# Gate, gelu and up products of the first two feed-forward groups in three passes instead of chunk by chunk

## The chip, the core and the metric

The kernel runs on one core of a Trainium2 chip. The metric is the device time of one execution, in microseconds (us). The engines are TensorE (PE), VectorE (DVE), ScalarE (ACT), GpSimd (POOL) and SyncE (SP, which issues the transfers). They run on their own and wait for one another by semaphores. Each engine executes its instructions in the order in which the program lists them.

## What is computed

One transformer block with adaptive layer norm: attention with 32 heads of width 16 over 2048 tokens of width 512, and then a gated feed-forward of width 1792.

```python
mod = (_silu(c) @ w_mod).reshape(c.shape[0], 6, 1, -1)     # sa, ca, ga, sb, cb, gb
h = _layernorm(x, axis=-1) * (1 + ca) + sa
x = x + ga * _A_ref(h, A_wqkv, A_wo)                        # softmax attention
h = _layernorm(x, axis=-1) * (1 + cb) + sb
x = x + gb * _B_ref(h, B_w_gate, B_w_up, B_w_down)
# _B_ref: _gelu(x @ w_gate) * (x @ w_up) @ w_down, gelu in its tanh form
```

## The kernel before

**Attention.** The queries are cut into six sets (`SETS`: three of 512 tokens, one of 256, two of 128). Eight head groups (`qd`) of four heads go over each set; one head group of one set is a unit. A unit of 512 queries has 16 rounds, one for each tile of 128 keys, and a round has four score blocks of 128x512, one for each head. PE writes the scores of three blocks into three PSUM banks (`ps_sc`, two such halves, used in turn), and one ACT instruction (line 1387, recorded by line 326) takes their exp into `E`, 1536 columns wide. Then PE multiplies by the values (`pv_mms`) into the accumulator `ps_pv`. At the end of a unit DVE copies the accumulator to `osb`, and the denominators go through DRAM and back by small transfers on SP's queue.

**Rounds on DVE.** Some rounds are taken off ACT. In the last four of the 16 rounds of keys, one bank of the three is given to DVE in four successive iterations; DVE computes the exp in bit arithmetic (line 1394: `dreg<-ps_sc`, `mreg<-ps_sc`, 128x512), and then makes four shifted copies of the whole round (`shift_task`, line 1476: `mreg<-dreg`, `mreg<-mreg`, 128x2048), each with its own value product (`ps_pv<-mreg,vs`). The iteration's exp on ACT is then 1024 wide. A round is started when DVE is free within 700 ns in the planner's model, fewer than `BACK` = 8 operations wait for DVE, and one of three buffers (`kq`) is free (lines 1358 to 1371). It is started at least `AHEAD` = 24 blocks before its turn. After the third set a further condition holds: little side work may be outstanding (`credit < CREDIT`).

**Side work.** Projections, output products and the feed-forward of the sets already finished run between the attention steps on PE, in one PSUM bank (`ps_mi`). They are generators (`plan`, from line 1118), paced by credit so that each is done by a due position in the sequence of score blocks. The feed-forward of group `gi` (`side_ffn`) runs while set `gi + 1` is in attention.

**The planner.** The whole order is fixed when the program is built: `stream` keeps a model of when each engine is free (`model`, `cost`, `probe`) and issues what the model has ready. DVE and ACT operations that are not urgent lie in a list of tasks (`task`); a task may have a condition and sets a key when it is recorded, and a generator may hold until a key is there (`until`). ACT's tasks are emptied ahead of each exp (lines 1385 and 1386). The order of the recorded instructions is the order on the chip; the times of the model are not.

**The feed-forward before.** `G(ci)` multiplies two gate columns blocks of 128 (`fc`), four matmuls of 512 columns each; DVE copies each from `ps_mi` to `g` (in `wreg`). Then four steps follow for the pair, as one task: `w = g*g`, `w = 0.0447 w + 1`, `w = w*g` on DVE, 1024 columns wide, and tanh on ACT. Tanh lies in the table that exp uses. `U(ci)` holds until the tanh is recorded, multiplies the two up blocks, and takes each out of PSUM by `(w + 1) * up` (line 1040); a last DVE product with `g` gives `prod` (line 1042). G of the next pair runs between G and U of a pair. For the first three groups (`flow`) the weights are streamed: gate and up each have two buffers of 256 columns (`wst`, in `mreg`), loaded one pair ahead, and the seven parts of the down weights go to `wdst`, four of which lie in the place of `wst`. Group 3 and later hold the weights in place. The final stage, after the last scores, uses the gelu of ACT itself, which lies in another table.

Of the kernel before, what the change touches and what calls it, by code (L numbers as in the profile page):

```python
# [5 lines left out]
ACT = mybir.ActivationFunctionType  # L6
ALU = mybir.AluOpType
# [6 lines left out]
P = 128  # L14
# [6 lines left out]
NDC = D // P  # L21
NFC = F // P
# [20 lines left out]
NS = 4  # L43
AHEAD = 24
FLOW = 3
URGENT = 9
LATE = 2
EARLY = 2
BACK = 8
END = (0, None)  # L50
# [14 lines left out]
class _Op:  # L65
    __slots__ = ("eng", "stream", "seq", "fn", "inc", "waits", "clock", "tag", "t1")

    def __init__(self, eng, stream, seq, fn):
        self.eng = eng
        self.stream = stream  # L70
        self.seq = seq
        self.fn = fn
        self.inc = False
        self.waits = {}
        self.clock = None
        self.tag = None


class _Recorder:


    def __init__(self, nc):
        self.nc = nc
        self.ops = []
        self.count = {}
        self.bystream = {}
        self.clock = {e: {} for e in ALLENG}
        self.hist = {}
        self.pitch = {}
        self.kind = {}  # L90
        self.sem = {}
        self.dry = False
        self.split = False
        self.probing = None
        self.free = {e: 700.0 for e in ALLENG}
        self.dma_free = self.pe_issue = self.pe_end = 0.0
        self.pe_mode = None
        self.tile_free = [0.0] * 16
        self.log = []

# [218 lines left out]
    def act(self, out, in_, func, bias=None, scale=1.0, accum=None):  # L319
        kw = {} if bias is None else {"bias": bias}  # L320
        wr = [out]
        if accum is not None:
            kw["accum_out"] = accum
            wr.append(accum)
        rd = [in_] + [a for a in (bias, scale) if isinstance(a, bass.AP)]
        return self.rec("act", lambda e: e.activation(out, in_, func, scale=scale, **kw), rd, wr,  # L326
                        cost=self.cost("act", out, [in_], "act"))

    def tt(self, eng, out, a, b, op):
        return self.rec(eng, lambda e: e.tensor_tensor(out, a, b, op), [a, b], [out],  # L330
# [88 lines left out]
class _Kernel(_Recorder):  # L419
# [78 lines left out]

    def prologue(self):
        sp, act, pe, dve, pool = "sp", "act", "pe", "dve", "pool"  # L500
        xv = self.A_x.rearrange("b (t p) d -> p (b t) d", p=P)
        wmv = self.w_mod.rearrange("(a p) n -> p a n", p=P)
        wqv = self.A_wqkv.rearrange("(a p) (k n) -> p a k n", p=P, k=3)
        wq4 = self.wqkv.rearrange("p a (k n) -> p a k n", k=3)
        self.dma(sp, self.xs[:, 0:2, :], xv[:, 0:2, :], "x0")
        self.dma(act, self.crow[0:1, :], self.c, "c")
        self.dma(act, self.xs[:, 2:4, :], xv[:, 2:4, :], "x1")
        for i, q in enumerate((sp, act)):
            self.dma(q, self.wmod[:, :, D * i:D * i + D], wmv[:, :, D * i:D * i + D], "wm%d" % i)
# [459 lines left out]
    def side_ffn(self, gi, part=None):  # L969

        q0, W = SETS[gi]
        n = W // P
        tiles = [q0 // P + i for i in range(n)]
        mi = self.mi[:, :]
        c0 = BCOL[gi]
        prod = self.prodT if W == 512 else self.prodL
        flow = gi < FLOW
        kpb = 512 // W
        chunks = []
        width = max(2, kpb)  # L980
        for a in range(0, NFC, width):
            chunks.append(range(a, min(NFC, a + width)))

        def load(x, ci):
            if flow and ci < len(chunks):
                v = (self.B_w_gate, self.B_w_up)[x].rearrange("(a p) n -> p a n", p=P)
                self.dma("sp", self.wst[x][ci % 2], v[:, :, 2 * P * ci:2 * P * ci + 2 * P], "st%d%d" % (x, ci % 2))

        def load_down(i):
            if flow:  # L990
                v = self.B_w_down.rearrange("(f p) n -> p f n", p=P)
                self.dma("sp", self.wdst[i], v[:, 2 * i:2 * i + 2, :], "sd%d" % i)

        yield from self.until(("ln2", gi))
        if flow:
            load(0, 0)
            load(1, 0)
        else:
            yield from self.until("weights")
        for h in range(2):  # L1000
            yield from self.side_t(lambda t: self.normed(gi, t), n, h,
                                   lambda dc: self.t2T[:, dc, c0:c0 + W], self.modB)

        def up(x, ci, sub):
            for s, fc in enumerate(sub):
                for dci in range(NDC):
                    if flow:
                        lhs = self.wst[x][ci % 2][:, dci, P * (fc % 2):P * (fc % 2) + P]
                    else:
                        lhs = self.up_w((self.wg, self.wu)[x], fc, dci)  # L1010
                    yield W, lambda s=s, lhs=lhs, dci=dci: self.mm(
                        mi[:, W * s:W * s + W], lhs, self.t2T[:, dci, c0:c0 + W], start=(dci == 0), stop=(dci == NDC - 1), whole=W == P)

        def G(ci):
            fcs = chunks[ci]
            m = len(fcs)
            g, w = self.gw[:, ci % 2, 0, 0:m * W], self.gw[:, ci % 2, 1, 0:m * W]
            load(0, ci + 1)
            for b0 in range(0, m, kpb):
                sub = fcs[b0:b0 + kpb]  # L1020
                yield from up(0, ci, sub)
                self.copy("dve", g[:, W * b0:W * (b0 + len(sub))], mi[:, 0:W * len(sub)])
                if b0 + kpb >= m and not self.dry:
                    self.task([lambda: self.tt("dve", w, g, g, ALU.mult),
                               lambda: self.ts("dve", w, w, GELU_C, 1.0, ALU.mult, ALU.add),
                               lambda: self.tt("dve", w, w, g, ALU.mult),
                               ("act", lambda: self.act(w, w, ACT.Tanh, scale=TANH_C0))], ("gelu", gi, ci))
                yield END

        def U(ci):  # L1030
            fcs = chunks[ci]
            m = len(fcs)
            g, w = self.gw[:, ci % 2, 0, 0:m * W], self.gw[:, ci % 2, 1, 0:m * W]
            yield from self.until(("gelu", gi, ci))
            load(1, ci + 1)
            for b0 in range(0, m, kpb):
                sub = fcs[b0:b0 + kpb]
                k = len(sub)
                yield from up(1, ci, sub)
                self.stt(w[:, W * b0:W * (b0 + k)], w[:, W * b0:W * (b0 + k)], 1.0, mi[:, 0:W * k], ALU.add, ALU.mult)  # L1040
                if b0 + kpb >= m:
                    self.tt("dve", prod[:, fcs[0]:fcs[0] + m, c0:c0 + W], w.rearrange("p (k n) -> p k n", k=m),
                            g.rearrange("p (k n) -> p k n", k=m), ALU.mult)
                yield END
        nch = len(chunks) if part is None else part
        for i in range(3):
            load_down(i)
        for ci in range(nch + 1):
            if ci < nch:
                yield from G(ci)  # L1050
                if ci >= nch - 2:
                    load_down(3 + ci - nch + 2)
            if ci >= 1:
                yield from U(ci - 1)
                if ci >= nch - 1:
                    load_down(5 + ci - nch + 1)
        if part is not None:
            yield from self.near_end(gi + 1, 6, self.mi[:, 0:P])
            if not self.dry:
                self.done(("part", gi))  # L1060
            return
        for i in range(n):
            for fc in range(NFC):
                yield 512, lambda i=i, fc=fc: self.mm(
                    mi, prod[:, fc, P * i:P * i + P], (self.wdst if flow else self.wd)[fc // 2][:, fc % 2, :], start=(fc == 0), stop=(fc == NFC - 1))
            self.down_fin(mi, tiles[i])
            yield END
        self.done(("ffn", gi))
# [6 lines left out]
    def urgency(self, tk):  # L1075
# [5 lines left out]
        if tk[1] is None or tk[1][0] != "shift":  # L1081
            return 1
        return 0 if self.plain[tk[1][1]] <= URGENT else 2

# [659 lines left out]
```

## Time and profile before

| | us |
|---|---|
| median of 3 runs | 865.73 (864.06 to 866.16) |
| profiled execution | 862.18 |
| its span, first to last instruction | 860.4 |
| ACT busy | 834.0 |
| PE busy | 797.4 |
| DVE busy | 694.8 |

A line of a group names the kernel's line, the engine, the operation, the tile written and the tiles read with their shapes, the count, then busy time, mean ns of one, and the idle time of the engine ahead of them with what ended it. Line 326 is the helper that records every ACT instruction, line 338, 343, 330 and 347 are DVE's helpers, line 313 that of the matmuls. Counts of the change's operations over the whole run, for three groups of which the change touches two:

| operation | shape | count | mean ns |
|---|---|---|---|
| ACT tanh, `wreg<-wreg` | 128x1024 | 21 | 1157 |
| DVE products, `wreg<-wreg` | 128x1024 | 42 | 680 |
| DVE scale and add, `wreg<-wreg` | 128x1024 | 21 | 421 |
| DVE product to `prod`, `hreg<-wreg` | 128x1024 | 21 | 692 |
| ACT table load | | 2 | 1283 |

The two table loads are at the start and ahead of the final stage. DVE exponentiates 192 + 96 score blocks, which are 72 rounds.

### The profile page before, as it was taken

Reading aid. Unit: us, or ns where it says so; the run is one execution under the profiler, and the core shown is the slowest. Engines: PE = TensorE matmul, PEld = TensorE weight load, DVE = VectorE, ACT = ScalarE, POOL = GpSimd, SP = SyncE. Lnnn points to the kernel's source line nnn. Section 1 sums busy time; section 2 is a strip of 40 time slices with the busy share of each in tenths; the row PEclk is TensorE's granted clock in tenths of the full one; section 3 lists DMA queues with packets and bytes.
Section 4 is the critical chain, followed back from the end, with each engine's and each line's share of the span. In section 5 each row is a group of like instructions: output and inputs, shape, how many; then the busy total and the mean of one; then the engine's idle time right before and its main releaser. Section 6 shows DMA issues by size and latency. Waiting matters only on the chain.

```text
span 860.4 us, 27593 instructions
## 1 busy us (share of the span) xinstructions
PE 797.4 (93%) x12434; PEld 285.5 (33%) x12434; DVE 694.8 (81%) x1339; ACT 834.0 (97%) x748; POOL 4.5 (1%) x12
## 2 busy tenths in 40 slices
PE   7889999999999899899999999999999889998988
PEld 3333332322222222222222222222343233354456
DVE  7865989989889989988899989989987663687255
ACT  6999999999999999999999999999999999999992
POOL 1000000000000000000000000000000000000000
PEclk9999999999999999999999999999999999999999
DMA  9000000000003111210002112120134231500000
GB/s 312 9 26 17 3 9 9 10 9 9 10 4 93 44 45 33 58 33 20 10 15 82 45 32 58 34 58 11 45 92 119 80 81 43 153 11 10 21 5 14
DMA packets 63807, 38.06 MB, mean 44 GB/s; under 512 B 17389, under 2 KB 61546, under 8 KB 63690
## 3 DMA queue, kind: packets, MB, share of 16 engines
q1 hardware_dynamic: 62888, 35.52, 14.8%
q8 instruction: 97, 1.59, 0.8%
q10 hardware_dynamic: 802, 0.79, 0.3%
q14 instruction: 20, 0.16, 0.1%
HBM read 33.68 MB, written 2.61 MB: 42 GB/s over the span
## 4 chain that ended last, share of the span: by engine, by line
ACT 82%; PE 8%; DVE 5%; DMA 3%; SPq 1%; issue 1%; ACTq 0%; DVEq 0%
ACT E L326 79%; PE ps_sc L313 4%; PE ps_mi L313 3%; ACT wreg L326 3%; PE ps_pv L313 1%; DMA rb<-scr_rec 1%; DMA scr_rec<-rden 1%; SPq L376 1%; DVE st L366 1%; DVE hreg L338 1%; DMA xs<-in_A_x_dram 1%; DVE nwt L330 0%; DVE wreg L338 0%; DVE dreg L338 0%; DVE mreg L338 0%
## 5 line engine op out<-in xcount | busy, mean ns | idle before, releaser
L326 ACT ACTIVATE E<-ps_sc 128x1536 bf16<-128x1536 f32 (+2 forms) x698 | 805.5, 1343 | 11.8 <-PE ps_sc L313 11.7
L313 PE MATMUL ps_sc<-qT,kmo 32*128 32x512 bf16 (+2 forms) x1408 | 178.7, 323 | 11.3 <-ACT E L326 9.8
L313 PE MATMUL ps_sc<-qT,kme 32*128 32x512 bf16 (+2 forms) x1344 | 172.8, 331 | 13.8 <-ACT E L326 11.1
L313 PE MATMUL ps_pv<-E,vaug 128*17 128x512 bf16 (+2 forms) x2352 | 171.0, 322 | 2.3 <-DVE vaug L347 1.0
L338 DVE TENSOR_SCALAR dreg<-ps_sc 128x512 uint16<-128x512 f32 x192 | 132.3, 690 | 33.1 <-PE ps_sc L313 30.4
L338 DVE TENSOR_SCALAR mreg<-dreg 128x2048 uint16<-128x2048 uint16 x192 | 124.9, 682 | 0.4 <-PE ps_pv L313 0.4
L313 PE MATMUL ps_mi<-wreg,mreg 128*32 128x512 bf16 (+2 forms) x1504 | 110.3, 370 | 11.6 <-DVE wreg L343 6.6
L313 PE MATMUL ps_pv<-mreg,vs 128*17 128x512 bf16 (+2 forms) x1344 | 100.8, 350 | 1.4 <-DVE mreg L338 1.2
L313 PEld LDWEIGHTS ps_sc<-qT,kmo 32*128 32x128 bf16 x1408 | 48.1, 91 | 125.3 <-ACT E L326 96.4
L313 PEld LDWEIGHTS ps_sc<-qT,kme 32*128 32x128 bf16 x1344 | 45.4, 91 | 130.7 <-ACT E L326 98.9
L313 PEld LDWEIGHTS ps_pv<-E,vaug 128*17 128x17 bf16 x2352 | 52.4, 89 | 85.8 <-issue 60.3
L338 DVE TENSOR_SCALAR mreg<-ps_sc 128x512 uint16<-128x512 f32 x96 | 66.3, 691 | 17.2 <-PE ps_sc L313 15.3
L338 DVE TENSOR_SCALAR mreg<-mreg 128x2048 uint16<-128x2048 uint16 x96 | 63.0, 684 | 0.0
L313 PEld LDWEIGHTS ps_mi<-wreg,mreg 128*32 128x32 bf16 (+1 forms) x1504 | 34.0, 95 | 62.5 <-issue 20.6
L347 DVE CAST wreg<-ps_mi 128x512 bf16<-128x512 f32 x51 | 35.0, 687 | 15.4 <-PE ps_mi L313 14.6
L343 DVE SCALAR_TENSOR_TENSOR wreg<-wreg,ps_mi 128x512 bf16<-128x512 bf16 x51 | 34.9, 685 | 13.4 <-PE ps_mi L313 7.8
L313 PEld LDWEIGHTS ps_pv<-mreg,vs 128*17 128x17 bf16 x1344 | 31.2, 89 | 31.2 <-DVE mreg L338 13.8
L313 PE MATMUL ps_mi<-hreg,wreg 128*32 128x512 bf16 (+1 forms) x496 | 39.5, 377 | 2.2 <-DVE hreg L338 1.0
L313 PE MATMUL ps_mi<-wo,onorm 128*32 128x512 bf16 x480 | 37.8, 383 | 0.1
L330 DVE TENSOR_TENSOR wreg<-wreg 128x1024 bf16<-128x1024 bf16 (+1 forms) x60 | 35.7, 603 | 0.7
L330 DVE TENSOR_TENSOR onorm<-osb,rb 128x512 bf16<-128x512 f32 (+2 forms) x43 | 23.5, 548 | 12.1 <-DMA rb<-scr_rec 11.8
L313 PE MATMUL ps_mi<-mreg,hreg 128*32 128x512 bf16 x384 | 32.5, 384 | 0.0
(147 smaller groups left out, 571.0 us busy)
## 6 DMA issues: line engine op xcount, KB each, us to landing
mreg<-in_B_w_up_dram SPq DMA_DIRECT2D x25, 256.0 KB, 3.2
mreg<-in_B_w_gate_dram SPq DMA_DIRECT2D x21, 256.0 KB, 3.0
rb<-scr_rec SPq DMA_DIRECT2D x96, 32.0 KB, 1.8
mreg<-in_B_w_down_dram SPq DMA_DIRECT2D x12, 256.0 KB, 2.7
dreg<-in_B_w_down_dram SPq DMA_DIRECT2D x9, 256.0 KB, 3.7
mreg<-in_w_mod_dram SPq DMA_DIRECT2D x1, 2048.0 KB, 11.5
out_dram<-xs SPq DMA_DIRECT2D x15, 128.0 KB, 1.7
xs<-in_A_x_dram SPq DMA_DIRECT2D x3, 512.0 KB, 8.2
```

The costliest lines, as they stand in the source:

```text
L313: return self.rec("pe", lambda e: e.matmul(out, lhsT, rhs, start=start, stop=stop, tile_position=tp), [lhsT, rhs], [out], cost=(n, int(rhs ...
L326: return self.rec("act", lambda e: e.activation(out, in_, func, scale=scale, **kw), rd, wr, cost=self.cost("act", out, [in_], "act"))
L330: return self.rec(eng, lambda e: e.tensor_tensor(out, a, b, op), [a, b], [out], cost=self.cost(eng, out, [a, b], "tt"))
L338: return self.rec(eng, lambda e: e.tensor_scalar(out, a, s1, s2, **kw), rd, [out], cost=self.cost(eng, out, [a], "ts") + (60 if len(rd) > ...
L343: return self.rec("dve", lambda e: e.scalar_tensor_tensor(out, a, s, b, op0=op0, op1=op1), rd, [out], cost=self.cost("dve", out, [a, b], " ...
L347: return self.rec(eng, lambda e: e.tensor_copy(out, in_), [in_], [out], cost=self.cost(eng, out, [in_], "ts"))
L366: return self.rec("dve", lambda e: e.bn_stats(out, in_), [in_], [out], cost=self.cost("dve", out, [in_], "bn"))
L376: return e.dma_start(out, in_)
```

## The change

For groups 0 and 1 (`gi < BATCH`), `side_ffn` no longer alternates G and U. A new generator, `batch`, goes over all seven pairs of gate blocks first; each block is copied by DVE from PSUM straight to its place in `prod`. When the last of the 14 is recorded, two ACT tasks are entered, each a gelu in place over seven blocks (128x3584). Then all seven pairs of up blocks follow; each block is taken out of PSUM by one DVE operation, `(up * 2) * prod`, in place. The up block `fc` holds until its half's gelu is recorded. The down products are as before.

The four `wst` buffers form one ring for the 14 loads, each issued two pairs ahead. The first two loads are issued behind the first three parts of the down weights, and the transposes of the group's input are moved into `batch`. Group 2 and later are as before. The planner's model adds 1290 ns where ACT goes from exp or tanh to gelu or back.

```diff
+BATCH = 2
...
-        return self.rec("act", lambda e: e.activation(out, in_, func, scale=scale, **kw), rd, wr,
-                        cost=self.cost("act", out, [in_], "act"))
+        cost = self.cost("act", out, [in_], "act")
+        if self.probing is None and func in (ACT.Exp, ACT.Tanh, ACT.Gelu_apprx_tanh):
+            if self.table not in (None, func == ACT.Gelu_apprx_tanh):
+                cost += 1290
+            self.table = func == ACT.Gelu_apprx_tanh
+        return self.rec("act", lambda e: e.activation(out, in_, func, scale=scale, **kw), rd, wr, cost=cost)
...
+        def batch():
+            nch = len(chunks)
+            flat = [self.wst[1][1], self.wst[1][0], self.wst[0][1], self.wst[0][0]]
+
+            def load_n(i):
+                if i < 2 * nch:
+                    v = (self.B_w_gate, self.B_w_up)[i // nch].rearrange("(a p) n -> p a n", p=P)
+                    c = 2 * P * (i % nch)
+                    self.dma("sp", flat[i % 4], v[:, :, c:c + 2 * P], "st%d%d" % divmod(i % 4, 2))
+
+            def act(a, b):
+                return ("act", lambda: self.act(prod[:, a:b, :], prod[:, a:b, :], ACT.Gelu_apprx_tanh))
+            load_n(0)
+            load_n(1)
+            for h in range(2):
+                yield from self.side_t(lambda t: self.normed(gi, t), n, h,
+                                       lambda dc: self.t2T[:, dc, 0:W], self.modB)
+            for i in range(2 * nch):
+                x, ci = divmod(i, nch)
+                load_n(i + 2)
+                for fc in chunks[ci]:
+                    if x:
+                        yield from self.until(("gelu", gi, fc * 2 // NFC))
+                    for dci in range(NDC):
+                        yield W, lambda i=i, fc=fc, dci=dci: self.mm(
+                            mi, flat[i % 4][:, dci, P * (fc % 2):P * (fc % 2) + P], self.t2T[:, dci, 0:W], start=(dci == 0), stop=(dci == NDC - 1))
+                    if x:
+                        self.stt(prod[:, fc, :], mi, 2.0, prod[:, fc, :], ALU.mult, ALU.mult)
+                    else:
+                        self.copy("dve", prod[:, fc, :], mi)
+                        if fc == NFC - 1 and not self.dry:
+                            for j in range(2):
+                                self.task([act(NFC // 2 * j, NFC // 2 * j + NFC // 2)], ("gelu", gi, j), self.after([("mid", gi)]))
+                            self.done(("mid", gi))
+                    yield END
+                if i >= 2 * nch - 4:
+                    load_down(i - 2 * nch + 7)
...
+        if gi < BATCH:
+            yield from batch()
+        for ci in range(nch + 1 if gi >= BATCH else 0):
```

## The prediction

> **What bounds the kernel now.** I read four views: the page's busy shares and the chain of waits, then the busy time by stretches, then ScalarE's (ACT) groups and timeline, then VectorE's (DVE) groups in the stretches that the change touches.
>
> ```profile
> PE 797.4 (93%) x12434; PEld 285.5 (33%) x12434; DVE 694.8 (81%) x1339; ACT 834.0 (97%) x748; POOL 4.5 (1%) x12
> ...
> ACT 82%; PE 8%; DVE 5%; DMA 3%; SPq 1%; issue 1%; ACTq 0%; DVEq 0%
> ```
>
> ```profile
> 268.00:396.00 128.00, 117.99 (x1452) 34.44 (x1451) 115.70 (x192) 127.98 (x117) 0.00 (x0) 1.00 0.17 48
> 396.00:466.00 70.00, 68.21 (x847) 19.42 (x847) 62.47 (x114) 69.99 (x65) 0.00 (x0) 1.00 0.08 21
> 480.00:592.00 112.00, 104.43 (x1285) 29.72 (x1281) 100.87 (x166) 112.00 (x102) 0.00 (x0) 1.00 0.15 41
> ```
>
> The columns of the stretches are PE, weight load, DVE, ACT and POOL busy, the clock, DMA share, GB/s. The gate/up work of the first two groups lies in 268-396 and 480-592 (that is where their 14 tanhs are); 396-466 has only down and output products. ACT is busy for the whole of all three (127.98 of 128, 69.99 of 70, 112.00 of 112), so here a microsecond of ACT is a microsecond of the kernel and nothing else is. DVE is at 90%, 89% and 90%: near full, and that matters for one reason only. The planner gives DVE whole rounds of four score blocks, exponentiated there by bit arithmetic, when DVE is free in its model. Each round is taken off ACT. So DVE time is worth ACT time at an exchange rate, and the change is a trade: it makes ACT dearer directly and gives DVE time back.
>
> **ACT's prices.**
>
> ```profile
> 316.62 1.16 ACT L326 ACTIVATE wreg<-wreg 128x1024 bf16<-128x1024 bf16 x1
> 317.57 2.47 ACT L326 ACTIVATE E<-ps_sc 128x1024 bf16<-128x1024 f32 x2
> 319.80 1.17 ACT L326 ACTIVATE wreg<-wreg 128x1024 bf16<-128x1024 bf16 x1
> ```
>
> ```profile
> 834.05 2.90 ACT L326 ACTIVATE E<-ps_sc 128x1536 bf16<-128x1536 f32 x2
> 836.71 0.75 ACT L326 ACTIVATE wreg<-wreg 128x512 bf16<-128x512 bf16 x1
> 837.23 1.57 ACT L326 ACTIVATE E<-ps_sc 128x1536 bf16<-128x1536 f32 x1
> 838.82 1.28 ACT L326 ACT_TABLE_LOAD   x1
> 840.11 0.20 ACT L326 ACTIVATE tcol<-tcol 128x1 f32<-128x1 f32 x1
> ```
>
> Columns: start, duration, then the instruction. Neighbours overlap, so what one costs is the distance to the next start. A 1536-wide exp: (836.71 - 834.05)/2 = 1.33 us. The pair at 317.57 is one exp of each width (2.23 us), so the 1024-wide one costs 2.23 - 1.33 = 0.90: **0.43 us for a block of 512**. A 1024-wide tanh: 317.57 - 316.62 = 0.95; the 512-wide one 837.23 - 836.71 = 0.52, again 0.43 per 512. The last three lines are the only switch from the exp table to the gelu table: without it the next start would be 837.23 + 1.33 = 838.56, with it 840.11, so **a switch costs 1.55 us**: the 1.28 us load and the lost overlap.
>
> Removed: 14 tanhs x 0.95 = -13.3 us. Added: 4 gelus of 7 x 512 = 3584 columns. No row has that width; from 1024 up by five blocks, 0.95 + 5 x 0.43 = 3.10, four of them 12.4. That gelu runs at the tanh's pace is taken from the final stage, where its 512-wide gelus take 0.60 us beside 0.59 for a plain copy of the same width. Added: switches. Both halves become ready at one point (all gate chunks recorded), and the planner empties ACT's task list before the next exp, so the two stand back to back: one switch in, one out, per group: 4 x 1.55 = 6.2. The switch back to exp has no row: below by the bare load (4 x 1.28 = 5.1), above by the same 1.55 (the load has to wait for the end of the gelu as it did for the exp). I take the upper, it is the one whole switch that was measured. **ACT's direct sum: -13.3 + 12.4 + 6.2 = +5.3 us** (from +4.2).
>
> The Trainium skill (ScalarE: Activation LUTs, "What ACT_TABLE_LOAD costs") speaks against this change: 1283 ns of load and about 1380 ns of drain, 2.66 us for every switch, while exp and tanh share a table. The load agrees with the 1.28 above; the drain doesn't: the activation behind the load starts 0.01 us after its end. By the page the switches would be an estimated 10.6 us, and the direct sum +9.7.
>
> **DVE's prices.**
>
> ```profile
> L338 DVE TENSOR_SCALAR dreg<-ps_sc 128x512 uint16<-128x512 f32 x38 | 26.2, 690 | 5.8 <-PE ps_sc L313 5.5
> L338 DVE TENSOR_SCALAR mreg<-dreg 128x2048 uint16<-128x2048 uint16 x36 | 23.6, 682 | 0.0
> L338 DVE TENSOR_SCALAR mreg<-ps_sc 128x512 uint16<-128x512 f32 x20 | 13.8, 690 | 2.8 <-PE ps_sc L313 2.3
> L338 DVE TENSOR_SCALAR mreg<-mreg 128x2048 uint16<-128x2048 uint16 x20 | 13.1, 686 | 0.0
> ...
> L330 DVE TENSOR_TENSOR wreg<-wreg 128x1024 bf16<-128x1024 bf16 x14 | 9.3, 679 | 0.1
> L330 DVE TENSOR_TENSOR hreg<-wreg 128x1024 bf16<-128x1024 bf16 x7 | 4.8, 692 | 0.2
> ...
> L338 DVE TENSOR_SCALAR wreg<-wreg 128x1024 bf16<-128x1024 bf16 x7 | 2.9, 419 | 0.0
> ```
>
> These are DVE's groups in 268-396. The last three are what goes: 9.3 + 4.8 + 2.9 = 17.0 us a group. All rows of the stretch add up to 124.4 us where 115.7 were busy, since neighbours overlap; at that ratio (0.93) it is 15.8 us, 31.6 for both. What stays is equal in number and price: one copy a gate chunk (684 ns) and one product with the PSUM an up chunk (683), now on the product tile. The four upper rows are the rounds: 58 exps and 56 shifts for 76.7 us, at 0.93 some 5.0 us a round. A round takes four blocks off ACT: 4 x 0.43 = **1.7 us**. So the freed DVE time could buy 31.6/5.0 = 6.3 rounds at most.
>
> Not all of it is to be had. The first up product is put into DVE's queue as soon as its matmuls are issued, and then waits for the first gelu: 1.55 + 3.10 us after ACT reaches it, less about 1 us for the matmuls and the copy ahead: some 3.5 us in which everything behind it on DVE waits (the shifts, the copies of finished accumulators, PE's value products on shifted rounds). Against that stand the waits for tanh that go (1.4 and 1.2 us in the two stretches). ACT itself does not starve: both halves of its score banks are filled before the gelus end.
>
> How many rounds DVE then takes I read from the middle stretch, whose other work is like what is left:
>
> ```profile
> L338 DVE TENSOR_SCALAR dreg<-ps_sc 128x512 uint16<-128x512 f32 x26 | 18.0, 691 | 4.0 <-PE ps_sc L313 3.7
> ...
> L338 DVE TENSOR_SCALAR mreg<-ps_sc 128x512 uint16<-128x512 f32 x12 | 8.3, 691 | 2.6 <-PE ps_sc L313 2.3
> ```
>
> 38 exps, 9.5 rounds in 70 us: one each 7.4 us, with other work at 24% of DVE's time. In 268-396 it is 14.5 rounds, one each 8.8 us, with other work at 35%; without the removed operations that is 22%. During the gelus and switches (2 x 3.10 + 2 x 1.55 = 9.3 us) no scores advance and no round starts. So the first stretch, some 130 us long, holds (130 - 9)/7.4 = 16.4 rounds, +1.9; the second, 112 us with 12.5 rounds now, (115 - 9)/7.4 = 14.3, +1.8. I take **4 more rounds**, between 0 and 6.3: 4 x 1.7 = -6.8 us.
>
> Costed at nothing: PE's four more value products a round (ps_pv<-mreg,vs, 100.8 us for 1344 matmuls, 16 a round: 1.2 us each, 5 in all), which lie beside an ACT that never waits; without that cover they are +5. The weight loads are as many as before, in another order: the down weights now go ahead of the first gate chunk on SP's queue, 3 us each to land, and only side work waits. The planner now also counts a table load at the start of the final stage, which may reorder it: between -1.3 and +1.3 (one load), taken as 0.
>
> **The sum.** +5.3 - 6.8 = **-1.5 us**. The profiled execution took 862.2 us (860.4 span and 1.8 around it), so 860.7 by that; it is 3.5 us below the median of the three runs, 865.7, and I put the forecast on the median: **864.2 us**. A measurement here tells 0.3%, 2.6 us, from no change.
>
> **The rivals.**
> A, *DVE's time converts fully*: all of the 31.6 us turns into 6.3 rounds, 1.7 x 6.3 = 10.7 less, 5.3 - 10.7 = -5.4: 860.3. For it: DVE fills to 90% in each stretch whatever else it does. Against: the wait for the gelu.
> B, *slower: the buffers decide, not DVE's time*. A round holds one of three buffers until its five value products are done, which needs its head pair's turn; and a round must be started 24 blocks ahead. So about three fit into a head pair's 64 blocks. Counting shifted products between accumulator copies, the pairs of 268-396 took 2, 3, 3, 3, 2 and those of 396-466 4, 3, 3: not far apart. If the buffers bind, only 0 to 2 more rounds are had and +5.3 is paid: +1.9 to +5.3, with one round +3.6: 869.3. It decides below 5.3/1.7 = 3.1 more rounds.
> C, *switching costs twice*: an exp comes between the two halves, 8 switches in place of 4: +6.2 on the forecast, 870.4. Against it: the emptying of the task list. The skill's drain would give nearly the same (an estimated +4.4).
>
> **Chances.** Forecast 40% (3 to 5 rounds: 862.5 to 865.9), A 22%, B 31%, C 7%. Faster by over 0.3%: A and the forecast's upper end, 0.31; slower: B below two rounds (0.24) and C, 0.31; within: 0.38. The range reaches to A and, above, to B's one round: 860.5 to 869.5.
>
> **What would show it.** Six table loads in place of two, four of them in two pairs round two gelus of 3.1 us each; DVE stalled 3 to 4 us behind the first; 76 rounds in place of 72 (304 score exps on DVE, now 192 + 96); ACT busy all through. Under 75 rounds B is right. I am wrong altogether if ACT shows idle time in the middle stretches, or if the rounds change after 660 us.

## The result and the profile after

| | before | changed |
|---|---|---|
| median, runs of one comparison | 864.98 us (9 runs) | 869.70 us (9 runs) |
| ratio | | 1.0052, 95% interval 1.0039 to 1.0065 |
| mean granted PE clock, run by run | 0.992 to 1.000 (the 67 runs beside the experiments below) | 0.977 to 0.988 |
| rounds on DVE | 72 | 75 |

The kernel became 4.7 us slower where 1.5 us faster was forecast. Ratios here and below leave out the runs of a second, slower state, so they are not exactly the quotients of the medians. The profiled execution of the changed kernel is its slowest, 874.2 us; its span is 872.5, 12.1 more than before. The profiled execution of the kernel before, 862.2 us, is under all nine runs of the comparison. So the two profiles lie further apart than the medians: they show where time goes, and not how much of the 4.7 us each place has. The busy shares and the chain on the page of the changed kernel:

```profile
PE 812.8 (93%) x12424; PEld 287.5 (33%) x12424; DVE 680.2 (78%) x1307; ACT 835.7 (96%) x742; POOL 4.5 (1%) x12
...
ACT 70%; PE 22%; DVE 5%; DMA 2%; issue 1%; SPq 0%; ACTq 0%; DVEq 0%
```

ACT's busy time grew by 1.7 us only; PE's share of the chain went from 8% to 22%. About the same three stretches of the work as before, moved by what they grew, the middle one taken further (before, ACT was busy for 20.00 of 20 us in 460 to 480, too) (columns: PE, weight load, DVE, ACT and POOL busy, clock, DMA share, GB/s):

```profile
268.00:396.00 128.00, 121.72 (x1472) 35.11 (x1472) 108.89 (x179) 127.26 (x113) 0.00 (x0) 0.97 0.15 42
396.00:480.00 84.00, 81.61 (x943) 22.42 (x947) 71.72 (x131) 79.66 (x73) 0.00 (x0) 0.94 0.11 31
480.00:600.00 120.00, 113.80 (x1324) 30.64 (x1312) 97.89 (x159) 114.18 (x101) 0.00 (x0) 0.91 0.15 41
```

Two things are to be seen. ACT is no longer busy throughout: 0.7, 4.3 and 5.8 us are idle, where it was full before. And the clock column, which was 1.00 in all three, is 0.97, 0.94 and 0.91. ACT's gelus in the first group, from its timeline:

```profile
318.64 1.28 ACT L332 ACT_TABLE_LOAD   x1
319.93 6.27 ACT L332 ACTIVATE hreg<-hreg 128x3584 bf16<-128x3584 bf16 x2
326.21 1.28 ACT L332 ACT_TABLE_LOAD   x1
327.50 2.79 ACT L332 ACTIVATE E<-ps_sc 128x1536 bf16<-128x1536 f32 x2
```

The block is as predicted: two gelus of 3.14 us each back to back, one load on either side, 8.86 us from the first load to the next exp (9.1 with the lost overlap ahead of it). What follows it was not. The second group's block in windows of 3.41 us, the grid on which the clock moves in the records:

```profile
521.60:525.01 3.41, 3.41 (x50) 1.11 (x47) 3.03 (x6) 3.38 (x3) 0.00 (x0) 1.00 0.05 10
525.01:528.42 3.41, 1.83 (x28) 0.54 (x28) 2.23 (x5) 3.41 (x2) 0.00 (x0) 1.00 0.03 2
528.42:531.83 3.41, 0.74 (x8) 0.00 (x0) 0.00 (x0) 3.39 (x4) 0.00 (x0) 0.50 0.43 115
531.83:535.24 3.41, 3.36 (x22) 0.50 (x22) 1.98 (x3) 2.60 (x3) 0.00 (x0) 0.50 0.04 12
535.24:548.90 13.66, 13.66 (x92) 2.35 (x88) 6.46 (x10) 9.72 (x9) 0.00 (x0) 0.50 0.06 17
548.90:552.31 3.41, 3.25 (x36) 0.81 (x32) 2.67 (x5) 2.87 (x4) 0.00 (x0) 1.00 0.00 0
```

In the second window PE is busy 1.83 of 3.41 us, and from the third on its clock is at 0.50, for 20.5 us. PE is then busy all the time (13.66 of 13.66) at half its rate, and it is ACT that waits for scores: it is busy for only 9.72 of 13.66 us. Why PE ran dry, in its timeline of that place:

```profile
526.83 0.39 PE L314 MATMUL ps_mi<-wreg,mreg 128*32 128x512 bf16 x4
528.02 1.15 PE L314 MATMUL ps_mi<-wreg,mreg 128*32 128x512 bf16 x12 [0.80 <-DVE hreg L348]
531.88 1.03 PE L314 MATMUL ps_sc<-qT,kme 32*128 32x512 bf16 x3 [2.72 <-ACT E L332]
```

While ACT is in the block no bank of scores comes free. The side bank is taken by an up block of which 12 of 16 matmuls are issued: the side work's credit was spent, and an open accumulation can take nothing else. So PE waits for the next exp, from 529.2 to 531.9. In the first group the side bank waits for the first product, and so for the first gelu, from 321.9 to 324.0; there the clock is at one half from 323.6 to 330.4.

The planner has a means against this that the text so far did not need: where PE's work in the last 3.413 us is under `FILL` = 4200 columns, it issues filler products on the identity, into a free bank (before, lines 1354 and 1433; 112 of them in the program). Full rate is taken here as 8192 columns in that time, 512 in 0.213 us; in the timelines one group of four quarter matmuls of 512 columns follows the other after 0.216 us. Through the gelus there is hardly a free bank. In the first group nine fillers run when the side bank is free at last, from 326.7 us on, but the clock was halved 3 us earlier; there it is back at 330.4.

The 12.1 us of the profiled execution divide so, by the distance from each ACT start to the next against the undisturbed distance: ACT's own work -0.2 (direct +4.9, three rounds -5.1), start and end +0.7, ACT's waits +11.7. Of the waits, 11.2 lie in three half-clock stretches: 0.8 behind the first block, 6.7 behind the second, and 3.7 between 463 and 474 us. The last is at no gelu: it lies between the output products of set 1 and the start of group 1's feed-forward. The kernel before issues seven fillers there, from 458 to 467 us; the changed kernel issues its first at 464, when the clock is halved already. Why the planner leaves them out is not shown.

Run by run, time follows the clock: 867.5 to 869.7 us at 0.986 to 0.988, 869.6 to 869.8 at 0.984, 870.2 to 870.4 at 0.982, 874.2 at 0.977. A line through the nine runs gives 861.8 at 0.998, where most runs of the kernel before lie (an extrapolation, outside the runs' clocks).

### The profile page after: what moved, and what is told of

Same layout as the page of the kernel before. It is cut to its first block, busy times and chain, and to the rows that moved or that the text cites. A ratio compares the mean times of both kernels' runs of the same rounds, so it can differ in the third digit from the quotient of the medians.

```text
span 872.5 us, 27529 instructions
## 1 busy us (share of the span) xinstructions
PE 812.8 (93%) x12424; PEld 287.5 (33%) x12424; DVE 680.2 (78%) x1307; ACT 835.7 (96%) x742; POOL 4.5 (1%) x12
## 4 chain that ended last, share of the span: by engine, by line
ACT 70%; PE 22%; DVE 5%; DMA 2%; issue 1%; SPq 0%; ACTq 0%; DVEq 0%
ACT E L332 67%; PE ps_sc L314 9%; PE ps_mi L314 7%; PE ps_pv L314 5%; ACT wreg L332 1%; ACT hreg L332 1%; DVE st L371 1%; DMA rb<-scr_rec 1%; DMA xs<-in_A_x_dram 1%; DVE mreg L343 1%; DVE dreg L343 1%; DVE hreg L343 1%; ACT L332 0%; DVE nwt L335 0%; DMA scr_rec<-rden 0%
## 5 line engine op out<-in xcount | busy, mean ns | idle before, releaser
L332 ACT ACTIVATE E<-ps_sc 128x1024 bf16<-128x1024 f32 (+2 forms) x698 | 800.8, 1325 | 21.8 <-PE ps_sc L314 21.1
L314 PE MATMUL ps_sc<-qT,kme 32*128 32x512 bf16 (+2 forms) x1344 | 181.8, 337 | 14.5 <-ACT E L332 11.9
L314 PE MATMUL ps_sc<-qT,kmo 32*128 32x512 bf16 (+2 forms) x1408 | 183.2, 324 | 10.2 <-ACT E L332 8.7
L343 DVE TENSOR_SCALAR dreg<-ps_sc 128x512 uint16<-128x512 f32 x200 | 137.7, 690 | 47.8 <-PE ps_sc L314 45.5
L343 DVE TENSOR_SCALAR mreg<-dreg 128x2048 uint16<-128x2048 uint16 x200 | 130.5, 682 | 2.7 <-PE ps_pv L314 2.7
L314 PE MATMUL ps_mi<-wreg,mreg 128*32 128x512 bf16 (+2 forms) x1504 | 115.6, 378 | 8.8 <-DVE hreg L348 3.0
L314 PE MATMUL ps_pv<-mreg,vs 128*17 128x512 bf16 (+2 forms) x1376 | 104.5, 354 | 2.3 <-DVE mreg L343 1.9
L335 DVE TENSOR_TENSOR onorm<-osb,rb 128x512 bf16<-128x512 f32 (+2 forms) x43 | 23.6, 550 | 11.5 <-DMA rb<-scr_rec 11.2
L352 DVE COPY osb<-ps_pv 128x512 f32<-128x512 f32 (+2 forms) x42 | 22.9, 545 | 7.9 <-PE ps_pv L314 7.6
L352 DVE CAST wreg<-ps_mi 128x512 bf16<-128x512 f32 x23 | 15.9, 691 | 15.6 <-PE ps_mi L314 15.4
L348 DVE SCALAR_TENSOR_TENSOR hreg<-ps_mi,hreg 128x512 bf16<-128x512 f32 x28 | 19.2, 686 | 6.6 <-PE ps_mi L314 4.3
```

The source lines that it names most:

```text
L314: return self.rec("pe", lambda e: e.matmul(out, lhsT, rhs, start=start, stop=stop, tile_position=tp), [lhsT, rhs], [out], cost=(n, int(rhs ...
L343: return self.rec(eng, lambda e: e.tensor_scalar(out, a, s1, s2, **kw), rd, [out], cost=self.cost(eng, out, [a], "ts") + (60 if len(rd) > ...
L348: return self.rec("dve", lambda e: e.scalar_tensor_tensor(out, a, s, b, op0=op0, op1=op1), rd, [out], cost=self.cost("dve", out, [a, b], " ...
L352: return self.rec(eng, lambda e: e.tensor_copy(out, in_), [in_], [out], cost=self.cost(eng, out, [in_], "ts"))
```

## The experiments

Each was compared with the kernel before on its own chip. Line numbers and edits are of the changed kernel unless said.

| run | rounds | median us | before us | ratio (95%) | clock of the runs |
|---|---|---|---|---|---|
| hold, fillers | 75 | 877.51 | 864.59 | 1.0131 (1.0072 to 1.0189) | 0.974 to 0.990 |
| hold, no fillers in it | 75 | 876.09 | 864.59 | 1.0114 (1.0075 to 1.0153) | 0.967 to 0.984 |
| tanh for gelu | 76 | 858.83 | 864.59 | 0.9943 (0.9916 to 0.9970) | 0.980 to 0.998 |
| before, four switches | 72 | 876.63 | 864.59 | 1.0141 (1.0126 to 1.0156) | 0.988 to 0.992 |
| hold and spend | 76 | 865.55 | 864.42 | 1.0011 (0.9998 to 1.0024) | 0.994 to 0.998 |
| the same, filling 4800 | 74 | 866.04 | 864.42 | 1.0018 (1.0006 to 1.0029) | 0.993 to 0.998 |
| before, filling 4800 | 72 | 866.79 | 864.42 | 1.0025 (1.0014 to 1.0035) | 0.992 to 0.997 |
| hold and spend, tanh | 76 | 862.89 | 864.42 | 0.9939 (0.9908 to 0.9970) | 0.976 to 0.998 |
| hold and spend, group 0 only | 74 | 864.18 | 865.16 | 0.9992 (0.9979 to 1.0006) | 0.992 to 1.000 |
| hold and spend, 1500 and 4500 | 76 | 862.38 | 865.16 | 0.9971 (0.9959 to 0.9984) | 0.996 to 0.998 |
| before, no fillers | 73 | 883.69 | 865.16 | 1.0202 (1.0172 to 1.0232) | 0.950 to 0.957 |
| before, no rounds in the second set | 49 | 903.97 | 865.16 | 1.0451 (1.0431 to 1.0472) | 0.994 to 0.998 |

**Is it the clock, and what starves PE?**

```diff
                     if x:
                         yield from self.until(("gelu", gi, fc * 2 // NFC))
+                        while not self.dry and self.probe(lambda: self.stt(...)) > self.now + 1000:
+                            self.holding = True
+                            yield None
+                        self.holding = False
...
+            if self.holding:
+                nxt.append(t + 100)
             virt = min(nxt) if nxt else t + 100
```

> Theory (clock): behind the gelus PE has no free PSUM bank and too little work, its clock is halved, and ACT then waits for scores; the ACT sum itself is about even. Here the first up products of each half wait in the planner until the gelu is nearly done, so the side bank is free for filler products meanwhile (12 more columns-blocks of 512 per group ahead of the up products). Theory: no half-clock stretch at the two gelu pairs, ACT idle back by 5 us or more, 865 to 867 us. Rival (price): the loss is the table switches against too few rounds on DVE; rounds are 75 as in the changed kernel, so 869 to 870.

877.5 us: the expected time was missed, and not on the rival's side either. The hold worked at the start of the block, but not behind it: the half-clock stretch of the first group now begins at 331.6 instead of 323.6, that of the second at 533.0 instead of 528.4, shortly behind the block. In the second block PE again stands with 12 of 16 matmuls of an up block issued, from 530.0 to 533.1. One part of the cause was treated, not the whole.

The second run differs by one condition on the fillers:

```diff
-            if self.short(t) > 0 and not self.open and gap > 213 and self.probe(
+            if not self.holding and self.short(t) > 0 and not self.open and gap > 213 and self.probe(
```

> The same hold, but no filler products during it: DVE is as free of the early product as in the run with fillers, PE is not. Theory (clock): half-clock stretches stay, 869 to 871. Rival (DVE stall: what hurts is that VectorE's queue is blocked by the first up product): 865 to 867, like the run with fillers.

876.1 us, clock down to 0.967, half-clock stretches of 6.8, 20.5 and 23.9 us in its profile. The stretches stayed, as expected, but the expected 869 to 871 us was missed, too. These two runs do not decide on the rival, VectorE's queue blocked by the first product: DVE still waits 1.9 us for the first gelu in both (1.8 in the changed kernel), since the hold ends when the gelu has 1 us left in the planner's model. The two don't differ by more than their scatter, so they don't tell the fillers' part apart. What they do show is that time goes with the clock: lines through their four runs each give 861.9 and 861.5 us at 0.998, the changed kernel's gives 861.8 (all three extrapolated, all with 75 rounds).

What was still missing was PE work that needs no bank of scores and no credit:

```diff
-                side = (ts <= t + 30 and (self.credit >= n / 2 or ...
+                side = (ts <= t + 30 and (self.credit >= n / 2 or (tq is not None and gap > 1400) or ...
```

> As the hold with fillers, and side products may also run without credit while ACT's next exp is more than 1.4 us off, so PE multiplies up blocks through the gelus instead of stopping when its credit is used up. 76 rounds on DVE. Theory (clock): no half-clock stretch at either gelu pair; ACT sum +5.3 - 4 x 1.7 = -1.5 us; if the stretch near 463 us (not at a gelu) stays too, 864 to 866; else 862 to 864. Rival (price of the switches alone): 868 or more whatever the clock.

865.6 us, clock 0.994 to 0.998: with the up products running on through the gelus, no half-clock stretch is left at either block, nor near 463 us. This is 3.5 us less in the ratio's terms (1.0052 against 1.0011), with the same gelus and switches; one more round on DVE, 1.7 us, is part of it. The rival of DVE's queue falls here: DVE waits the same 1.9 us for the first gelu, and the half-clock stretches are gone. The theory holds for the clock, but the time expected without the stretch near 463 us, 862 to 864, was missed: ACT's own work is 1.8 us under that of the kernel before, as summed in advance (-1.5), and its waits are 4.7 us longer. Nor were the extrapolated 861.8 us reached at a clock of 0.998 (four runs, 865.2 on average). Where the waits are, in the timeline of this run (one of six such places):

```profile
442.70 0.82 PE L316 MATMUL ps_mi<-wo,onorm 128*32 128x512 bf16 x12
443.10 0.68 DVE L354 COPY osb<-ps_pv 128x512 f32<-128x512 f32 x1
...
443.84 0.39 PE L316 MATMUL ps_pv<-E,vaug 128*17 128x512 bf16 x4 [0.32 <-DVE osb L354]
444.16 0.60 PE L316 MATMUL ps_sc<-qT,kmo 32*128 32x512 bf16 x6
444.59 1.02 ACT L334 ACTIVATE E<-ps_sc 128x1024 bf16<-128x1024 f32 x1 [0.68 <-PE ps_sc L316]
```

A unit ends on shifted products of a round, late; DVE then copies the accumulator, the next unit's value product stands at the head of PE's queue until it is done, and the scores that ACT needs are behind it. Six waits of 0.58 us or more stand behind such a copy here, two in the kernel before. What puts them there was not tried.

The opposite test takes the fillers from the kernel before and nothing else:

```diff
-FILL = 4200
+FILL = 0
```

> The kernel before without the planner's filler products (target 0; 1 filler left of 112), 73 rounds, nothing else changed. Theory (clock): PE's work in some stretches of 3.4 us falls under about 0.4 of its full rate, the clock is halved there and ACT waits for scores: clock under 0.98, 875 us or more. Rival (fillers and clock don't matter to a kernel bound by ACT): 862 to 866.

883.7 us, and the clock 0.950 to 0.957. ACT's waits for scores in its profile, and in that of the kernel before (columns: total us, times, longest):

```profile
ACT E L326 <- PE ps_sc L313: 27.7, 39, 2.1
```

```profile
ACT E L326 <- PE ps_sc L313: 11.7, 14, 2.1
```

Work that computes nothing is worth 18 us here, to a kernel whose bound is another engine, and without a gelu. Of the 882.0 us of the profile, 91 are at half clock (1 us in the kernel before), among them 10 us from 465 on, the place near 463 of the changed kernel. The planner's order changes a little with the fillers, too (73 rounds, worth 1.7 us the other way), so not every microsecond is shown to be the clock's.

Raising the target everywhere is no remedy in itself:

> The same with the planner's filling target raised from 4200 to 4800 columns in 3.4 us everywhere; 74 rounds. Theory (clock): hardly a half-clock stretch left (mean clock 0.996 or more); ACT sum +5.3 - 2 x 1.7 = +1.9 us, 865 to 868. Rival (price alone): above 869.

> Control: the kernel before with the filling target at 4800; 72 rounds as before. Theory: nothing to win where the clock was never halved, 864 to 866. If the fillers cost time by themselves: 867 or more.

866.0 and 866.8 us. In the first, the edits of the hold-and-spend run with `FILL = 4800`, one stretch of 6.8 us near 669 us remains. The expected time of the first was met, with 74 rounds, one fewer than in the changed kernel: 1.0018 against 1.0052 is 2.9 us, although ACT's own work is 1.7 us more. So the rounds do not make that difference; the clock, 0.993 to 0.998, is back. The control is 0.25% (0.14 to 0.35%) slower than the kernel before, between its two expectations. Its trace does not show that fillers cost time by themselves: with 220 fillers instead of 112, the last table load is at 838.13, 0.7 us earlier than before (838.82), and 1.0 us of tanh has moved behind it. So up to there the fillers cost some 0.3 us at most in these profiles. What is longer is the final stage, where ACT waits 5.91 us in one place (2.94 before) and the clock is halved from 851.5 to 854.9:

```profile
838.13 1.28 ACT L326 ACT_TABLE_LOAD   x1
...
850.64 0.81 ACT L326 ACTIVATE wreg<-ps_sc,modB 128x128 bf16<-128x128 bf16 x2 [5.91 <-PE ps_sc L317]
```

**What a table switch costs.**

```diff
-                return ("act", lambda: self.act(prod[:, a:b, :], prod[:, a:b, :], ACT.Gelu_apprx_tanh))
+                return ("act", lambda: self.act(prod[:, a:b, :], prod[:, a:b, :], ACT.Tanh))
```

> Tanh in place of the gelu in the three-pass form (the output is then another function): no table switch, 76 rounds on DVE. ACT sum: -0.9 - 4 x 1.7 = -7.7 us. If switches cost 1.55 us each and the clock holds because the block is 3.1 us shorter: 857 to 859. If the clock is halved all the same: 860 to 863. Rival (switches are cheap, the rest of the form is what costs): 868 or more.

The median, 858.8, lies in the range of the first case, but its ten runs cover both: 855.1 to 857.4 us at clocks of 0.994 and more, 858.8 at 0.990, 862.3 to 868.1 at 0.986 and less. In one program, with one order of instructions, 10.5 us lie between the run at 0.998 (855.1) and one at 0.980 (865.5).

> The hold-and-spend kernel with tanh in place of the gelu (the output is then another function): the same 76 rounds and no table switch. Difference to it at equal clock: four switches. By one row of the trace before, 4 x 1.55 = 6.2 us; by the skill's 2.66, 10.6. Time 857 to 859.

The median, 862.9, is above the range, again by the clock: four runs at 0.996 to 0.998 took 853.8 to 855.3, eight at 0.976 to 0.986 took 861.3 to 868.3. The three runs at 0.998 average 854.2; the four of the hold-and-spend run with gelu at 0.998 average 865.2. That is 11.0 us for four switches, 2.75 each, not 1.55. ACT's own work differs by 6.0 in the two profiles, that is 1.5 a switch, as in the row of the kernel before; the other 5 us are left over by subtraction, and since no run of the tanh kernel at full clock was profiled, which waits they are is not shown. The Trainium skill (ScalarE: Activation LUTs, "What ACT_TABLE_LOAD costs") gives 2.66 us a switch, of which 1.38 is a drain. Its total is near the 2.75 of this comparison, but ACT's timeline has no such drain. This is seen best where almost nothing else happens, in the kernel before with one gelu of one column in each of the two groups (the planner counts 1290 ns a switch here, too):

```diff
+                if ci == nch - 1 and gi < 2 and not self.dry:
+                    self.task([("act", lambda: self.act(self.tcol[:, 0:1], self.tcol[:, 0:1], ACT.Gelu_apprx_tanh))], ("sw", gi))
```

> The kernel before with one gelu of a single column behind the last gate chunk of groups 0 and 1, that is four table switches and nothing else; 72 rounds. At 1.55 us a switch plus 0.2 for each activation: +6.6 us, 871 to 872. At the bare load of 1.28: +5.5. With a drain of 1.38 beside each load (the skill's figure): +11, 876.

```profile
357.28 4.43 ACT L331 ACTIVATE E<-ps_sc 128x1024 bf16<-128x1024 f32 x4
361.73 1.28 ACT L331 ACT_TABLE_LOAD   x1
363.02 0.20 ACT L331 ACTIVATE tcol<-tcol 128x1 f32<-128x1 f32 x1
363.23 1.28 ACT L331 ACT_TABLE_LOAD   x1
364.52 2.79 ACT L331 ACTIVATE E<-ps_sc 128x1536 bf16<-128x1536 f32 x2
```

Load, activation, load and exp follow within 0.02 us of one another: no drain but the missing overlap. The four switches add 5.9 us to ACT's own work, near the expected 6.6. The expected 871 to 872 us was missed all the same: the kernel is 12 us slower (876.6, the time that the drain would have given), at a clock of 0.988 to 0.992 and with 7.5 us more of ACT waits in its profile, which has half-clock stretches of 3.4 and 6.8 us at 492 and 768 us. So a switch costs ACT 1.5 us, and these kernels lost 2.75 and 3.0 us a switch. How much of the rest is the order behind a switch and how much the clock was not separated.

**What a round on DVE is worth.** In the kernel before, no candidate rounds in the second set:

```diff
-                if u not in units[:2] and r * (512 // u[3]) >= T0]
+                if u not in units[:2] and r * (512 // u[3]) >= T0 and u[0] != (1,)]
```

> The kernel before with no round on DVE in the second set of queries: 49 rounds instead of 72. It measures what a round is worth. At 1.7 us each, 23 rounds are +39 us: 903 to 904. If the hand-over of the accumulator takes back a part (about 1 us where a pair ends on shifted products), 10 to 20% less: 895 to 900.

903.97 - 865.16 = 38.8 us for 23 rounds, **1.69 us each**: the exchange rate of the prediction, with nothing taken back.

**One group, and a version below both.** `BATCH = 1` on the hold-and-spend kernel:

> Hold-and-spend with the new form for group 0 alone (group 1 as before): two switches instead of four, 74 rounds on DVE. ACT sum: half of +5.3, that is +2.7, less 2 x 1.7 = -0.7 us. If switches and rounds have the prices taken, 863 to 866, level with the kernel before; if a switch costs 2.66, +1.5, 865 to 867.

864.2 us, level with the kernel before as expected. Then the planner's price of a switch was set nearer to the measured one, and a little more filling allowed:

```diff
-                cost += 1290
+                cost += 1500
...
-FILL = 4200
+FILL = 4500
```

> Hold-and-spend for both groups, the planner counting 1500 ns for a switch instead of 1290 and filling to 4500 columns; 76 rounds. Looked for: a version below both kernels. ACT sum -1.5 us; with fewer half-clock stretches than the run with the target at 4200, 863 to 865; if the waits where a head pair's accumulator is handed over stay, 865 to 866.

**862.38 us, 0.29% (0.16 to 0.41%) under the kernel before** and below the changed kernel. This is 2.5 us, where the prediction had 1.5 for the change itself. Which of its two edits did it was not tried apart. Its windows at the second block:

```profile
519.20:522.61 3.41, 3.04 (x50) 1.00 (x42) 3.34 (x7) 3.38 (x3) 0.00 (x0) 1.00 0.05 8
522.61:526.02 3.41, 3.03 (x48) 1.00 (x45) 3.41 (x7) 3.41 (x2) 0.00 (x0) 1.00 0.19 57
526.02:529.43 3.41, 2.10 (x32) 0.67 (x32) 1.70 (x4) 3.39 (x3) 0.00 (x0) 1.00 0.43 128
529.43:532.84 3.41, 2.90 (x33) 0.85 (x33) 1.59 (x3) 3.41 (x4) 0.00 (x0) 1.00 0.04 12
```

The gelus lie between 521.6 and 527.9 here, and PE is busy for 2.10 us or more of each window; the clock stays at 1.00 and ACT is full. Its own work is 1.9 us under the kernel before and its waits 1.2 us longer.

## Why the prediction was wrong

**ACT's direct sum** was right: +5.3 predicted, +4.9 in the changed kernel's profile (two blocks of 9.1 us against 13.3 of tanh). The two gelus stood back to back; rival C did not occur.

**DVE's relief** was right in kind and near in size: 4 more rounds were forecast, 3 came:

```profile
L343 DVE TENSOR_SCALAR dreg<-ps_sc 128x512 uint16<-128x512 f32 x200 | 137.7, 690 | 47.8 <-PE ps_sc L314 45.5
...
L343 DVE TENSOR_SCALAR mreg<-ps_sc 128x512 uint16<-128x512 f32 x100 | 69.0, 691 | 26.9 <-PE ps_sc L314 25.2
```

300 blocks are 75 rounds, at 1.69 us each. The idle time at the end of the lines, 74.7 us against 50.3 before, is mostly DVE waiting for scores. The stall behind the first gelu, put at 3.5 us, was 1.8 in the first group and none in the second. ACT's own work came to -0.2 instead of -1.5, so this term explains 1.3 us of the 6.2 between forecast and median.

**The step that failed** is the cover: PE's work was "costed at nothing", to lie "beside an ACT that never waits", and "ACT itself does not starve: both halves of its score banks are filled before the gelus end". The prediction named +5 us as the price without that cover, and gave this case no chance. The banks were filled; but that is just why PE had next to nothing to do. It ran under the work that holds its clock, the clock went to one half for 6.8 and 20.5 us, and ACT starved behind the block, not in it. A third half-clock stretch, near 463 us, has no gelu, and why it came with the change stays open. The profile before showed a clock of 1.00 in every row, and this was read as a given of the chip, not as a result of the program's fillers. No rival named it.

The runs answer this by putting PE's work back. Beside ACT's own work by each profile (as reckoned above, against the kernel before) stands the time by the ratio, in us:

| run | ACT's own work | time | clock of the runs |
|---|---|---|---|
| changed | -0.2 | +4.5 | 0.977 to 0.988 |
| hold, fillers | -0.2 | +11.3 | 0.974 to 0.990 |
| hold, no fillers in it | -0.2 | +9.9 | 0.967 to 0.984 |
| before, four switches | +5.9 | +12.2 | 0.988 to 0.992 |
| before, no fillers | -1.7 | +17.5 | 0.950 to 0.957 |
| hold and spend | -1.8 | +1.0 | 0.994 to 0.998 |
| the same, filling 4800 | +1.5 | +1.6 | 0.993 to 0.998 |
| hold and spend, group 0 only | -0.9 | -0.7 | 0.992 to 1.000 |
| hold and spend, 1500 and 4500 | -1.9 | -2.5 | 0.996 to 0.998 |

Where the clock is kept, the time is within 0.6 us of ACT's own sum in three of four runs; hold and spend has the waits at the accumulator on top, which no run took away alone. Where it is not kept, the time is 5 to 19 us above the sum.

The time, 869.7, is beside rival B's 869.3, but that is chance: B's mechanism did not decide, since the rounds were 75 and the ACT sum about even.

**The price of a switch** in the whole kernel was set too low. With 1.55 us the row of ACT's timeline was read rightly (1.5 in the runs), but the kernels lost 2.75 and 3.0 us a switch, through waits that no row of the profile before could show. The 2.66 us that the Trainium skill (ScalarE: Activation LUTs, "What ACT_TABLE_LOAD costs") gives for a switch is nearer to that, though not by the drain it names.

The signs given in advance named ACT idle time in the middle stretches as what would show the prediction wrong altogether; it was there: 0.7, 4.3 and 5.8 us.

## What to carry to other kernels

A long instruction on the bounding engine is also a hole in the work of every engine that feeds it: count what TensorE can still do in that hole, bank by bank and credit by credit, before costing it at nothing. A granted clock of 1.00 is something that a program maintains; when a change moves PE work, look at PE's work per 3.4 us, not at its mean. And when an operation goes to a free engine at a rate worked out from rows, measure that rate by taking a number of them away: here it came out as 1.69 us where 1.7 was worked out.

## What the runs showed of the hardware

The clock changes on a grid of 3.413 us. Counting the matmul columns of each such window in the fourteen profiles (a matmul on a quarter of the array as a quarter, 8192 columns being full rate), 42 of the 43 windows at full clock with under 0.34 were followed by one at half clock, and none of those over 0.40; between the two both occurred. The Trainium skill (TensorE: Matmul & The Clock Gate, "Part 1: The HAM clock gate (the "warmup" mystery)") names the same window and an idle one as the condition; here windows in which PE was busy for more than half of the time by the profile (1.83 of 3.41 us) were enough. At half clock a window that is busy throughout counts about 0.50 at most; no window under 0.35 was followed by full clock, and from 0.36 to 0.42 both occurred: a PE that waits in turns with ACT stays there, for up to 24 us. A microsecond at half clock costs this kernel about a third of a microsecond: in the runs of tanh for gelu 0.018 of mean clock, some 31 us at half rate, is 10.5 us of time (865.5 against 855.1).
